# A 16-row copy of 1 KiB rows within SBUF, placed ahead of the alpha load on the ACT queue of a streaming add kernel

## Chip, cores and metric

The kernel runs on one core of a Trainium2 chip. The time is device microseconds of one execution; a kernel is quoted by the median of its runs. "Profile" and "trace" mean the record of one execution by the hardware profiler; its span is about 1.8 us shorter than the device time of the same execution. A run that is over 1.5% above the fastest run of the same kernel is marked "slow" and left out of the ratios.

Some words used below: SP, ACT, VectorE and PE are engines of the core. Transfers are issued on a queue, here that of SP or that of ACT; the core's 16 DMA engines carry out the transfers of both (the page gives both queues as shares of the same 16). A packet is one record of a DMA engine in the trace; here it is one row of a transfer, or a 4-byte completion, which reports that an engine's share of a transfer is done. A transfer lands when all its completions have arrived. A turn is the time from one packet of the ACT queue to the next on the same DMA engine. SBUF is the core's working memory, PSUM the memory that matmuls write to.

## The reference

```python
B, S, D = 512, 32, 640          # x, fx: bfloat16; alpha: one bfloat16 number
def reference(x, fx, alpha):
    return x + alpha * fx
```

Two inputs of 21 MB are read and one output of 21 MB is written. There is one multiply-add per element, so the kernel should run at the speed of its transfers.

## The kernel before

Each of the 128 partitions owns 81,920 elements. They are cut into five chunks of 16,384 elements, that is, rows of 32 KiB per partition and 4 MiB per transfer. All large loads and stores are issued on the SP queue. The one number alpha is loaded on the ACT queue, spread to 128 partitions by a one-column matmul and copied from PSUM to `a_f`, which every multiply-add needs.

```python
def alpha_to_lanes(nc, consts, psum, alpha, eng):
    a_1 = consts.tile([1, 1], alpha.dtype, name="a_1")
    eng.dma_start(out=a_1[:], in_=alpha[None, :])
    ones = consts.tile([1, P], alpha.dtype, name="ones")
    nc.vector.memset(ones[:], 1.0)
    a_ps = psum.tile([P, 1], F32, name="a_ps")
    nc.tensor.matmul(a_ps[:], ones[:], a_1[:], start=True, stop=True)
    a_f = consts.tile([P, 1], F32, name="a_f")
    nc.vector.tensor_copy(out=a_f[:], in_=a_ps[:])
    return a_f
# ... cut ...
    xs = ctx.enter_context(tc.tile_pool(name="xs", bufs=4))
    fs = ctx.enter_context(tc.tile_pool(name="fs", bufs=2))
    ctx.enter_context(tc.manual_schedule())
    a_f = alpha_to_lanes(nc, consts, psum, alpha, nc.scalar)
# ... cut: load_x, load_f, store issue on nc.sync; compute is x_t = f_t * a_f + x_t on VectorE ...
    load_x(0)
    load_f(0)
    load_x(1)
    load_f(1)
    load_x(2)
    compute(0)
    load_f(2)      # needs the buffer of f_t(0): waits for the end of compute(0)
    store(0)
    load_x(3)
    compute(1)
    load_f(3)
    store(1)
    load_x(4)      # needs the buffer of x_t(0): waits for store(0)
    compute(2)
    load_f(4)
    store(2)
    compute(3)
    store(3)
    compute(4, 2)  # in two halves
    store(4, 0, 2)
    store(4, 1, 2)
```

Of the kernel before, what the change touches and what calls it, by code (L numbers as in the profile page):

```python
# [1 line left out]

# [4 lines left out]

ACT = mybir.ActivationFunctionType
ALU = mybir.AluOpType
F32 = mybir.dt.float32  # L10
BF16 = mybir.dt.bfloat16

CHUNK = 16384


def alpha_to_lanes(nc, consts, psum, alpha, eng):

    P = nc.NUM_PARTITIONS
# [11 lines that stand above are left out]
@with_exitstack  # L30
def kernel(
    ctx: ExitStack,
    tc: tile.TileContext,
    x: bass.AP,
    fx: bass.AP,
    alpha: bass.AP,
    out: bass.AP,
):
    nc = tc.nc
    P = nc.NUM_PARTITIONS  # L40
    xv = x.flatten_outer_dims().rearrange("(p n) d -> p (n d)", p=P)
    fxv = fx.flatten_outer_dims().rearrange("(p n) d -> p (n d)", p=P)
    ov = out.flatten_outer_dims().rearrange("(p n) d -> p (n d)", p=P)
    F = xv.shape[1]
    K = F // CHUNK
    assert K * CHUNK == F and K == 5

    consts = ctx.enter_context(tc.tile_pool(name="consts", bufs=1))
    psum = ctx.enter_context(tc.tile_pool(name="psum", bufs=1, space=bass.MemoryType.PSUM))
    xs = ctx.enter_context(tc.tile_pool(name="xs", bufs=4))  # L50
    fs = ctx.enter_context(tc.tile_pool(name="fs", bufs=2))
    ctx.enter_context(tc.manual_schedule())

    a_f = alpha_to_lanes(nc, consts, psum, alpha, nc.scalar)
    xt, ft = {}, {}

    def load_x(k):
        xt[k] = xs.tile([P, CHUNK], x.dtype, tag="x", name="x_t")
        nc.sync.dma_start(out=xt[k][:], in_=xv[:, bass.ts(k, CHUNK)])  # L59

    def load_f(k):
        ft[k] = fs.tile([P, CHUNK], fx.dtype, tag="f", name="f_t")
        nc.sync.dma_start(out=ft[k][:], in_=fxv[:, bass.ts(k, CHUNK)])

    def compute(k, parts=1):
        n = CHUNK // parts
        for j in range(parts):
            s = bass.ts(j, n)
            nc.vector.scalar_tensor_tensor(  # L69
                out=xt[k][:, s],  # L70
                in0=ft[k][:, s],
                scalar=a_f[:],
                in1=xt[k][:, s],
                op0=ALU.mult,
                op1=ALU.add,
            )

    def store(k, j=0, parts=1):
        n = CHUNK // parts
        nc.sync.dma_start(  # L80
            out=ov[:, k * CHUNK + j * n : k * CHUNK + (j + 1) * n],
            in_=xt[k][:, bass.ts(j, n)],
# [8 lines that stand above are left out]
    load_f(2)  # L91
# [5 lines that stand above are left out]
    load_x(4)  # L97
# [5 lines that stand above are left out]
    compute(4, 2)  # L103
    store(4, 0, 2)
    store(4, 1, 2)


# [1 line left out]
_INS = ['x', 'fx', 'alpha']  # L109
_OUTS = [((512, 32, 640), 'bfloat16')]  # L110


# [23 lines left out]
```

## Time and profile before

| | before |
|---|---|
| time, median of the first 3 runs | 152.83 us (152.47 to 152.9) |
| span of the profiled run | 150.6 us |
| share of 16 DMA engines' span filled by the SP queue | 98.0% |
| bytes, mean rate | 62.92 MB, 418 GB/s |
| VectorE busy | 86.9 us, 58% |
| first multiply-add starts | 22.84 us |

These lines are from the page of the kernel before. The DMA row has one digit per fortieth of the span: the busy share of the 16 DMA engines in tenths. Below it are the counts of packets, and then the two queues, q1 (SP) and q10 (ACT).

```profile
DMA  6999999999999999799999999999999999999994
DMA packets 2306, 62.92 MB, mean 418 GB/s; under 512 B 258, under 2 KB 258, under 8 KB 258
q1 hardware_dynamic: 2304, 62.92, 98.0%
q10 hardware_dynamic: 2, 0.00, 0.0%
```

The reader sees a kernel bound by its DMA engines: they are full between the first and the last slice. The chain of waits of the same run (start, length, what) shows where that work is waited for.

```profile
1.16 21.55 DMA f_t<-in_fx_dram
22.84 17.30 DVE x_t L69
40.16 21.99 DMA f_t<-in_fx_dram
62.24 17.29 DVE x_t L69
79.55 41.16 DMA f_t<-in_fx_dram
120.91 8.75 DVE x_t L69
```

Three of the five loads of `f_t` carry the chain, the first, third and fifth; a multiply-add appears between them only where its end releases a buffer for a load (at 40.16 and 79.55). The load that begins at 40.16 is the third load of f, and it can only be issued when the first multiply-add has freed its buffer.

The timeline of the start (start, length, engine, line, operation, then in brackets the idle time before and what ended it) shows how alpha arrives.

```profile
0.73 0.38 SPq L59 DMA_DIRECT2D x_t<-in_x_dram  x1
0.73 0.49 ACTq L20 DMA_DIRECT2D a<-in_alpha_dram  x1
1.92 0.16 PE L24 MATMUL a_ps<-a,ones 1*128 1x1 bf16 x1 [1.92 <-DMA a<-in_alpha_dram]
2.11 0.16 DVE L26 COPY a_f<-a_ps 128x1 f32<-128x1 f32 x1 [1.13 <-PE a_ps L24]
22.84 17.28 DVE L69 SCALAR_TENSOR_TENSOR x_t<-f_t,a_f,x_t 128x16384 bf16<-128x16384 bf16 x1 [20.57 <-DMA f_t<-in_fx_dram]
```

Alpha's issue and the first load's issue begin together at 0.73. Alpha is on VectorE's side at 2.3 us, and VectorE then idles for 20.57 us until the first `f_t` lands.

### The profile page before, as it was taken

To read this page: it belongs to the slowest core of one execution; us is meant where nothing else is said; L and a number is where in the kernel's file an instruction comes from. 1 tells how busy PE (TensorE), PEld (TensorE's weight loads), DVE (VectorE), ACT (ScalarE), POOL (GpSimd) and SP (SyncE) were. 2 spreads that over 40 slices of the span, in tenths; PEclk is the share of its full clock that TensorE was granted. 3 is DMA by queue.
4 is the path that set the end of the run, shared out by engine and by line. 5 is a ranking of instruction groups with operands and counts; after the bars stand their busy time and mean duration, and the time that the engine had idled before them with its cause. 6 is when DMAs were issued, how large, how long until landed. Compare 5 with 4: busy or idle time off the path is not lost.

```text
span 150.6 us, 85 instructions
## 1 busy us (share of the span) xinstructions
PE 0.2 (0%) x1; PEld 0.1 (0%) x1; DVE 86.9 (58%) x8; POOL 0.2 (0%) x4
## 2 busy tenths in 40 slices
PE   0000000000000000000000000000000000000000
PEld 0000000000000000000000000000000000000000
DVE  0000009999679998499991006999900089997000
POOL 0000000000000000000000000000000000000000
DMA  6999999999999999799999999999999999999994
GB/s 200 444 453 435 418 418 418 418 444 453 444 453 435 418 418 418 339 444 470 418 418 418 418 418 435 435 435 453 426 435 444 418 418 435 435 435 405 426 444 205
DMA packets 2306, 62.92 MB, mean 418 GB/s; under 512 B 258, under 2 KB 258, under 8 KB 258
## 3 DMA queue, kind: packets, MB, share of 16 engines
q1 hardware_dynamic: 2304, 62.92, 98.0%
q10 hardware_dynamic: 2, 0.00, 0.0%
HBM read 41.94 MB, written 20.97 MB: 418 GB/s over the span
## 4 chain that ended last, share of the span: by engine, by line
DMA 56%; DVE 29%; DVEq 6%; issue 0%; SPq 0%
DMA f_t<-in_fx_dram 56%; DVE x_t L69 29%; DVEq L131 6%; SPq L59 0%; DVEq L69 0%
## 5 line engine op out<-in xcount | busy, mean ns | idle before, releaser
L69 DVE SCALAR_TENSOR_TENSOR x_t<-f_t,a_f,x_t 128x16384 bf16<-128x16384 bf16 (+1 forms) x6 | 86.6, 14439 | 49.5 <-DMA f_t<-in_fx_dram 49.5
L26 DVE COPY a_f<-a_ps 128x1 f32<-128x1 f32 x1 | 0.2, 159 | 1.1 <-PE a_ps L24 1.1
L22 DVE MEMSET ones<- 1x128 bf16 x1 | 0.2, 165 | 0.8 <-PEq L120 0.8
L24 PE MATMUL a_ps<-a,ones 1*128 1x1 bf16 x1 | 0.2, 159 | 1.9 <-DMA a<-in_alpha_dram 1.9
L120 POOL MEMSET const-bfloat16-1.0<- 128x1 bf16 x1 | 0.1, 102 | 0.0
L120 POOL MEMSET const-uint8-127<- 128x1 uint8 x1 | 0.1, 102 | 0.0
L24 PEld LDWEIGHTS <-ones 1*128 1x128 bf16 x1 | 0.1, 100 | 1.0 <-DVE ones L22 1.0
L120 POOL MEMSET const-float32-0.0<- 128x1 f32 x1 | 0.1, 99 | 0.2 <-issue 0.2
L120 POOL MEMSET const-float32-1.0<- 128x1 f32 x1 | 0.1, 99 | 0.0
## 6 DMA issues: line engine op xcount, KB each, us to landing
x_t<-in_x_dram SPq DMA_DIRECT2D x5, 4096.0 KB, 34.8
f_t<-in_fx_dram SPq DMA_DIRECT2D x5, 4096.0 KB, 32.1
out_dram<-x_t SPq DMA_DIRECT2D x4, 4096.0 KB, 36.5
out_dram<-x_t SPq DMA_DIRECT2D x2, 2048.0 KB, 15.2
a<-in_alpha_dram ACTq DMA_DIRECT2D x1, 0.0 KB
```

Source lines behind the costliest of these rows:

```text
L22: nc.vector.memset(ones[:], 1.0)
L24: nc.tensor.matmul(a_ps[:], ones[:], a_1[:], start=True, stop=True)
L26: nc.vector.tensor_copy(out=a_f[:], in_=a_ps[:])
L69: nc.vector.scalar_tensor_tensor(out=xt[k][:, s], in0=ft[k][:, s], scalar=a_f[:], in1=xt[k][:, s], op0=ALU.mult, op1=ALU.add,)
L120: nc = _bacc.Bacc("TRN2", target_bir_lowering=False, num_devices=1)
L131: with _tile.TileContext(nc) as tc:
```

## The change

A tile of 16 rows of 512 bfloat16 numbers is cleared and copied to another tile on the ACT queue, before alpha's load is issued there. Nothing reads the copy. It has the form of a warm-up of the queue; its effect on the result is none.

```diff
     ctx.enter_context(tc.manual_schedule())
 
+    w_a = consts.tile([16, 512], x.dtype, name="w_a")
+    nc.vector.memset(w_a[:], 0.0)
+    w_b = consts.tile([16, 512], x.dtype, name="w_b")
+    nc.scalar.dma_start(out=w_b[:], in_=w_a[:])
     a_f = alpha_to_lanes(nc, consts, psum, alpha, nc.scalar)
```

## The prediction

> **What bounds the kernel now.** The page gives a span of 150.6 us. In its forty slices the 16 DMA engines are in the top tenth nearly throughout, and the one big queue (q1) fills 98.0% of 16 engines' span: 62.92 MB at a mean of 418 GB/s. VectorE is busy 86.9 us (58%), nothing else matters. The chain of waits agrees: f_t loads 56%, then VectorE 29%; its last pieces are the landing of the fifth f_t at 120.72 us, two half multiply-adds (17.4 us), and the last store until 150.6. The DMA engines work through VectorE's part of the chain too (windows: share 1.01, 0.98, then 0.80 in the last 11 us, the drain).
>
> **What the change adds, removes, moves.** Nothing is removed; the order on SP, PE and POOL is the same, and on SP the same waits stand in front of the same transfers (DMA semaphores are handed out in rotation; none of the new waits can still be open at 40 us).
> - VectorE: a memset of 16 rows. That of `ones` took 0.165 us; estimate 0.2-0.3 us, while VectorE otherwise idles until 22.84.
> - ACT: its queue waits for that memset and issues the copy first. The alpha issue began at 0.73 us and took 0.49; I expect the copy's issue at about 1.1 and alpha's at 1.6.
> - Engines: 16 packets of 1 KiB, one per engine, and 16 completion packets. A 32 KiB packet takes 1.23 us in steady state; by bytes 1 KiB is 0.04 us, so my estimate is at most 0.1 us per engine, during start-up (windows: share 0.81 and 0.70 in the first 4 us).
> - Alpha lands later. Before, its matmul started at 1.92 us, 1.19 us after alpha's issue began. The Trainium skill (DMA: Bandwidth & Descriptors, "Queues, rings and completion order") says an engine goes round its queues packet by packet, so the ACT transfers pass between SP's packets instead of behind SP's whole queue. This trace doesn't show that yet: alpha's packets ran ahead of the first load. Estimate 2.8 us plus one to two 32 KiB packets: matmul at 3 to 6 us, a_f 0.2-0.4 us later.
>
> **How much is on the critical path.** The first multiply-add needs f_t(0), x_t(0) and a_f; f_t(0) releases it at 22.84, a_f is ready at 2.3. Alpha has about 20 us of slack and should lose 1 to 4. Only the DMA time counts: at most 0.1 us. SBUF addresses move by 2 KiB per partition, which should cost nothing.
>
> **Predicted time.** 152.9 us, range 152.2 to 153.7: before plus under 0.1 us, and the scatter of its runs (152.47 to 152.9). Faster by over 2%: 0.02. Within 2%: 0.95. Slower by over 2%: 0.03.
>
> **What would show each step.**
> - Page: DMA packets 2306 + 32 = 2338, q10 with 34; VectorE x9; q1 still about 98%.
> - Timeline: matmul at 3 to 6 us; first multiply-add still at about 22.9, released by f_t, not a_f.
> - Chain: same three members and shares; f_t(4) landing near 120.8.
> - Waits: SP's as before within a few tenths of us.
>
> **What would make it wrong.**
> - If alpha stood behind all loads already queued (five are issued in the first 3.2 us, about 50 us of traffic), the first multiply-add would be up to 25 us late; SP's waits on VectorE would grow and the engines run dry.
> - If a small packet put the engines out of step so that the rate changed for long: each 1% is 1.5 us.
> - If the copy's issue held up SP's first loads: 0.5 us at most.

## The result

The changed kernel takes 152.81 us (152.65 to 152.85, 4 runs), the kernel before 152.81 us (152.47 to 152.9, 4 runs). The ratio is 1.0002, with a 95% interval of 0.9985 to 1.0019. A ratio here is the mean time of one kernel's fast runs over that of the other's fast runs of the same rounds, so it is not quite the ratio of the quoted medians.

These lines of the changed kernel's page answer to those of before.

```profile
DMA  6999999999999999899999999999999999998993
DMA packets 2339, 62.93 MB, mean 417 GB/s; under 512 B 275, under 2 KB 291, under 8 KB 291
q1 hardware_dynamic: 2304, 62.92, 97.8%
q10 hardware_dynamic: 34, 0.02, 0.0%
```

The ACT queue has 34 packets instead of 2: 16 of 1 KiB, 16 completions, and alpha's two. (The thirty-third additional packet is an instruction fetch on another queue.) The SP queue is unchanged. The chain of waits has the same members at nearly the same times:

```profile
1.16 21.67 DMA f_t<-in_fx_dram
22.96 17.30 DVE x_t L74
40.28 22.04 DMA f_t<-in_fx_dram
62.41 17.30 DVE x_t L74
79.72 41.22 DMA f_t<-in_fx_dram
121.06 8.75 DVE x_t L74
```

The timeline of the start is where the change shows:

```profile
0.84 0.27 DVE L56 MEMSET w_a<- 16x256 uint32 x1 [0.84 <-PEq L125]
1.14 0.56 ACTq L58 DMA_DIRECT2D w_b<-w_a  x1
1.73 0.85 ACTq L20 DMA_DIRECT2D a<-in_alpha_dram  x1
10.37 0.16 PE L24 MATMUL a_ps<-a,ones 1*128 1x1 bf16 x1 [10.37 <-DMA a<-in_alpha_dram]
22.96 17.29 DVE L74 SCALAR_TENSOR_TENSOR x_t<-f_t,a_f,x_t 128x16384 bf16<-128x16384 bf16 x1 [12.24 <-DMA f_t<-in_fx_dram]
```

Alpha's matmul starts at 10.37 us instead of 1.92, which is 8.45 us later. The first multiply-add still starts on the landing of `f_t`, 0.12 us later than before. The idle time that VectorE spends just before it has only been split: 12.24 us there, and 9.31 us before the copy to `a_f`.

So the forecast of the time held, but one number in it did not: I had expected the matmul at 3 to 6 us. The experiments ask why alpha came so much later than I thought, how late it might have come without cost, and whether the copy itself costs anything. That the time was forecast rightly doesn't test the number for alpha: 12.24 us of VectorE's wait were left, so alpha could have come up to 12 us later still without delaying the first multiply-add.

### The profile page after: what moved, and what is told of

The parts are those of the page before. It is cut to its first block, busy times and chain, and to the rows that moved or that the text cites. A ratio compares the mean times of both kernels' runs of the same rounds, so it can differ in the third digit from the quotient of the medians.

```text
span 151.0 us, 87 instructions
## 1 busy us (share of the span) xinstructions
PE 0.2 (0%) x1; PEld 0.1 (0%) x1; DVE 87.1 (58%) x9; POOL 0.2 (0%) x4
## 3 DMA queue, kind: packets, MB, share of 16 engines
q1 hardware_dynamic: 2304, 62.92, 97.8%
## 4 chain that ended last, share of the span: by engine, by line
DMA 56%; DVE 29%; DVEq 6%; SPq 0%; issue 0%
DMA f_t<-in_fx_dram 56%; DVE x_t L74 29%; DVEq L136 6%; SPq L64 0%; DVEq L74 0%
## 5 line engine op out<-in xcount | busy, mean ns | idle before, releaser
L24 PE MATMUL a_ps<-a,ones 1*128 1x1 bf16 x1 | 0.2, 160 | 10.4 <-DMA a<-in_alpha_dram 10.4
```

## The experiments

Twelve experiments were run, all with correct results: ten variants, one of them on two chips, and the changed kernel once more. The kernel before was run beside them on the same chip, and each ratio is against those runs. Five of the twelve are a single run each; they serve for their traces, and their times are quoted only as a check.

### Why alpha is late

The trace records when each DMA packet moved its data. Taken from these records, the starts of the ACT queue's packets in us from the span's start (a range covers 16 engines):

```
                 copy data     copy completion  alpha data  alpha completion
before           -             -                1.58        1.59
change           5.91 - 6.62   7.16 - 7.87      8.62        9.84
late (no copy)   -             -                4.74        5.96
SP queue, both:  first 32 KiB packets from 1.74 on, the second ones from about 3.5 on;
                 median length of a 32 KiB packet 1.213
```

In the changed kernel alpha passes three further packets behind the first, and they stand about one large SP packet apart: 1.25, then about 1.2 to 1.3 (the records don't say which engine alpha's packet ran on), then 1.22 us. My estimate had counted one or two. The theory that follows from it: an engine gives each queue one packet in turn, a completion is a packet of its own, and on top of that the first ACT packet must wait for what SP has already handed to the engine. The rival is that the copy's own work or its mere presence delays alpha.

**Order swapped.** Alpha first, the copy behind it (this edit and the next two are shown against the changed kernel).

```diff
-    <the copy>
     a_f = alpha_to_lanes(nc, consts, psum, alpha, nc.scalar)
+    <the copy>
```

> The same copy, but behind alpha on the ACT queue instead of ahead of it. If alpha's lateness (matmul at 10.4 us after the change, 1.92 before) comes from its place in the queue and from arriving after the engines filled, the matmul is back at 1.9 to 2.1 us, and the copy itself still lands only at 6 to 9 us. If the copy's mere presence slows alpha, the matmul stays well over 3 us. Time the same as before within 0.5% in both.

```profile
1.95 0.16 PE L24 MATMUL a_ps<-a,ones 1*128 1x1 bf16 x1 [1.95 <-DMA a<-in_alpha_dram]
```

The matmul was at 1.95 us. The copy's data moved at 7.16 to 7.81 us and the copy landed at about 9.6 us, a little later than expected. The time was 152.99 us, one run, beside 153.35 for the kernel before. So the copy's presence doesn't delay alpha; being issued behind it does. The single time shows no loss.

**Alpha late, no copy.** Alpha's transfer waits for two memsets, so its issue begins at 1.16 us rather than 0.73.

```diff
-    nc.scalar.dma_start(out=w_b[:], in_=w_a[:])        # and w_b is gone
+    nc.vector.memset(a_1[:], 0.0)                      # in alpha_to_lanes, before the load
     eng.dma_start(out=a_1[:], in_=alpha[None, :])
```

> No copy at all; alpha's transfer only waits for two VectorE memsets, so it is issued at about 1.2 to 1.5 us instead of 0.73. Theory (a packet that comes after SP's first load was issued gets its first turn only after about four 32 KiB packets, and each further packet, the completion included, costs one more 32 KiB packet): alpha's data packet at about 6 us, its completion 1.2 us later, matmul at 7 to 8.5 us. Rival (the lateness is the copy's own cost, and alpha waits for the copy): matmul at 2.4 to 3 us. Time as before within 0.5%.

```profile
1.16 0.49 ACTq L21 DMA_DIRECT2D a<-in_alpha_dram  x1
6.33 0.16 PE L25 MATMUL a_ps<-a,ones 1*128 1x1 bf16 x1 [6.33 <-DMA a<-in_alpha_dram]
```

The matmul was at 6.33 us, between the two expectations but far from the rival's 3 us. An issue 0.43 us later costs alpha 4.4 us without any copy, because before the change alpha's packet left at 1.58 us, just ahead of the first SP packet at 1.74. So about half of the change's 8.45 us comes from losing that race, and about half from two more turns for the copy and an entry one turn later than here (why it was one turn later was not found). My theory had put alpha's data at 6 us and it came at 4.74: the wait for the first turn was over-sized by one packet. Time 152.43 us, one run.

**128 rows instead of 16.** The copy then has eight data packets of 1 KiB per engine.

```diff
-    w_a = consts.tile([16, 512], x.dtype, name="w_a")
+    w_a = consts.tile([128, 512], x.dtype, name="w_a")     # w_b0 likewise
```

> The copy with 128 rows of 1 KiB instead of 16, still ahead of alpha: 8 data packets per engine instead of 1. Theory (the engine takes one 1 KiB packet, then one 32 KiB packet, in turn): 7 more turns of 1.22 us, so the matmul at 18 to 20 us. Rival (an engine drains several small descriptors in one turn): matmul at 10.4 to 12 us. Time as before within 0.6% in both, as the first multiply-add starts at about 23 us.

```profile
17.58 0.16 PE L24 MATMUL a_ps<-a,ones 1*128 1x1 bf16 x1 [17.58 <-DMA a<-in_alpha_dram]
```

The matmul was at 17.58 us, a little under the theory's band and far from the rival's. The packet records say how the turns went: the first packets of the first five rows start at 5.91, 7.16, 8.41, 9.67 and 10.92 us, one turn of 1.25 us each. Between 12.2 and 13.0 us, on each engine, the sixth and the seventh follow each other within about 0.05 us. That is where the first load of x ends, so SP's packet between them is its own 4-byte completion: a turn is one packet, whatever its size. That short turn is 1.2 us less than a full one, which puts the matmul under my band. Time 153.31 us against 153.35, one run each.

**The first load in 8 KiB rows.** The changed kernel, with `load_x(0)` as four transfers.

```diff
-    load_x(0)
+    xt[0] = xs.tile([P, CHUNK], x.dtype, tag="x", name="x_t")
+    for q in range(4):
+        n = CHUNK // 4
+        nc.sync.dma_start(out=xt[0][:, bass.ts(q, n)], in_=xv[:, q * n : (q + 1) * n])
```

> The change as it is, but the first load of x in four transfers of 8 KiB rows instead of one of 32 KiB rows. Theory (each turn costs one SP packet of whatever size): a turn costs about 0.31 us instead of 1.22, so the matmul at 3.5 to 5.5 us. Rival (a fixed latency of an ACT transfer beside SP traffic): matmul still near 10 us. Time as before within 0.7%.

```profile
6.89 0.16 PE L24 MATMUL a_ps<-a,ones 1*128 1x1 bf16 x1 [6.89 <-DMA a<-in_alpha_dram]
```

The matmul was at 6.89 us, so neither expectation was met. The turns shrank as the theory says: from the copy's first data packet at 5.24 us to the last packet of alpha at 6.36 took 1.1 us, where the change took 3.9. But the first packet still had to wait until 5.24 us. The wait for the first turn is not a count of packets: about 10 SP packets per engine had started by then, instead of about 3. Time 152.69 us, one run.

**The first load in 2 KiB rows,** four such transfers and one of 24 KiB rows, to see what that first wait is.

```diff
-    load_x(0)
+    for lo, hi in ((0, 1024), (1024, 2048), (2048, 3072), (3072, 4096), (4096, CHUNK)):
+        nc.sync.dma_start(out=xt[0][:, lo:hi], in_=xv[:, lo:hi])
```

> The change, with the first load of x in four transfers of 2 KiB rows and one of 24 KiB rows, to see what sets how soon the first ACT packet gets a turn. With 32 KiB and with 8 KiB rows it was 4.8 and 4.1 us after the copy's issue, though engines had passed 3 packets in one case and about 10 in the other. Theory A (it waits for bytes that SP has already committed, about 64 to 96 KiB per engine; here only 16 KiB per transfer and engine): copy's packets at 2.5 to 4.0 us. Theory B (a fixed time of 3.6 to 4.8 us beside a busy queue): at 4.7 to 5.9 us. Time as before within 1% in both.

```profile
5.00 0.16 PE L24 MATMUL a_ps<-a,ones 1*128 1x1 bf16 x1 [5.00 <-DMA a<-in_alpha_dram]
```

The copy's data packets started at 3.32 to 3.9 us and the matmul at 5.00 us, as theory A has it. On the mean of the engines, SP had by then begun about 32 KiB, which is two of its small transfers. In the other runs it had begun 70 to 114 KiB where the ACT transfer was issued at about 1.15 us, 142 where it was issued at 2.60 (order swapped) and 166 where it was issued at 3.95 (the run with a hundred times the bytes, below). A fixed time is excluded by these traces. That an ACT transfer that arrives late waits for what SP has already committed fits them, but is not shown by itself. I did not find one number for how much that is; this part stays open. The kernel took 154.0 us in its one run, 1% more than the runs of before beside it (median 152.5), with its first `f_t` landing at 24.28 us. This was not repeated.

### How late alpha may come

**Alpha on the SP queue behind the second load of x,** with no copy:

```diff
-    a_f = alpha_to_lanes(nc, consts, psum, alpha, nc.scalar)
...
     load_x(1)
+    a_f = alpha_to_lanes(nc, consts, psum, alpha, nc.sync)
```

> The kernel before, with alpha's load moved from the ACT queue to the SP queue, behind the second load of x, to see how late alpha may come. It should land at about 32.5 us, so the first multiply-add starts at about 33 us instead of 22.9. Theory (what counts is whether the DMA engines still have work when the third load of f is issued; a first-in-first-out estimate from 9.83 us per 4 MiB load and 17.29 us per multiply-add gives room until an alpha at 33 us): time as before, 152.8, at most +0.6 us. Rival (the room is the 20.5 us that VectorE waits for f_t, as my prediction had it): 10 us later, about 163 us.

```profile
32.47 17.29 DVE L68 SCALAR_TENSOR_TENSOR x_t<-f_t,a_f,x_t 128x16384 bf16<-128x16384 bf16 x1
```

The first multiply-add started at 32.47 us. Two of the five runs were slow (156.19 and 156.41); the three fast ones were 153.84, 155.61 and 156.08 us, against 152.89 (152.62 to 154.21) for the kernel before. The ratio of the fast runs is 1.0196 (1.0136 to 1.0255), at the limit of 2% and so unclear. The rival's +10 us is excluded. The theory's "at most +0.6" is wrong too. Because of the scatter it was run again on another chip:

> The kernel with alpha behind the second load of x on the SP queue again, on another chip perhaps, since its times scattered (153.8 to 156.4) where others agree within 1 us. If it lies on the edge at which the engines just run dry before the third load of f, +1 to +3.5 us and again a wide scatter; if that scatter was the chip's, it settles near +1 us (its profile then: third f_t landing 1.2 us later). The rival of my prediction, +10 us, is already excluded.

Again the times scattered: 153.23, 153.94 and 154.53 us, and a slow run of 155.77, against 152.50 (152.25 to 152.91); ratio of the fast runs 1.0086 (1.0039 to 1.0133). In both profiles the third `f_t` lands about a microsecond later than before (63.3 and 63.1 us, before 62.1). The engines hardly stop, but the load comes so late that its packets begin on engines with nothing else queued: in the first of the two runs it was issued at 49.78 us, and its first packets, from 50.76 us on, took 1.5 to 1.9 us, where the median is 1.213. This is about the edge. The fast runs of the two series cover 2.2 and 1.3 us; the kernel before covered 1.6 and 0.7 beside them, and 2.1 on a third chip. In each series the profiled run was the fastest one, so the traces don't show where the others lost their time; this stays open.

**Alpha behind the second load of f,** ten microseconds later:

```diff
     load_f(1)
+    a_f = alpha_to_lanes(nc, consts, psum, alpha, nc.sync)
```

> The same with alpha behind the second load of f: it should land at about 42.3 us, the first multiply-add at about 43. Theory: beyond 33 us the time follows alpha one for one, so +9 to +11 us, about 163 us, with the DMA engines idle for about 10 us before the third load of f. Rival (room is 20.5 us): +20 us, about 173.

The time was 163.8 us (163.51 to 164.38), ratio 1.0706 (1.0653 to 1.0759), slower. The start of the first multiply-add in the timeline, the issue of the third load of f, and the DMA row of the page:

```profile
42.25 17.29 DVE L68 SCALAR_TENSOR_TENSOR x_t<-f_t,a_f,x_t 128x16384 bf16<-128x16384 bf16 x1
59.56 0.33 SPq L62 DMA_DIRECT2D f_t<-in_fx_dram  x1
```
```profile
DMA  7999899999994028989999999999999999999994
```

The hole in slices 13 to 16 is the loss. The table of stretches (length, the busy time of the engines, the granted clock, the DMA share, GB/s) gives its size:

```profile
40.00:51.00 11.00, 0.16 (x1) 0.00 (x0) 8.91 (x2) 0.00 (x0) 1.00 0.98 423
51.00:60.00 9.00, 0.00 (x0) 0.00 (x0) 9.00 (x2) 0.00 (x0) 1.00 0.00 0
60.00:74.00 14.00, 0.00 (x0) 0.00 (x0) 14.00 (x1) 0.00 (x0) 1.00 1.00 374
```

From 51 to 60 us not a byte moved while VectorE worked on the first chunk, because `load_f(2)` was waiting for that chunk's buffer. The multiply-add was 19.4 us late (42.25 against 22.84), and the kernel lost 0.0706 of about 153 us, or 10.8. So 8.6 us of the delay was free. In the kernel before, the same load had its buffer 19.4 us earlier:

```profile
40.16 0.33 SPq L63 DMA_DIRECT2D f_t<-in_fx_dram  x1
```

**The change grown threefold and eightfold in rows:** three copies of 128 rows ahead of alpha.

```diff
-    w_a = consts.tile([16, 512], x.dtype, name="w_a")
+    w_a = consts.tile([128, 512], x.dtype, name="w_a")
     nc.vector.memset(w_a[:], 0.0)
-    w_b = ...; nc.scalar.dma_start(out=w_b[:], in_=w_a[:])
+    w_b0, w_b1, w_b2 = ...; the same copy into each of the three
```

> The change grown: three copies of 128 rows of 1 KiB ahead of alpha, 0.4 MB in all. By bytes they are about 1 us of the engines. Theory of turns: 24 data and 3 completion packets per engine, then alpha's two, 28 further turns of 1.22 us after about 6 us: matmul at 39 to 42 us, first multiply-add at about 41, and by the estimate of first-in-first-out that is 7 to 9 us more than before, 160 to 162 us. Rival (only bytes count): about 153.9 us. If small packets are drained several per turn: matmul under 16 us and time about 153.9.

```profile
38.03 0.16 PE L24 MATMUL a_ps<-a,ones 1*128 1x1 bf16 x1 [38.03 <-DMA a<-in_alpha_dram]
38.42 17.29 DVE L78 SCALAR_TENSOR_TENSOR x_t<-f_t,a_f,x_t 128x16384 bf16<-128x16384 bf16 x1
```
```profile
DMA  7999999999999089989999999999999999999993
```

The time was 160.25 us (159.34 to 160.8), ratio 1.0463 (1.0403 to 1.0523), slower. The matmul came about a microsecond before the band, for the short turns seen above. The first multiply-add was 15.6 us late and the kernel lost 0.0463 of about 153 us, or 7.1; again 8.5 us of the delay was free. Two ways of making alpha late, through two queues, give the same room. The copies' own engine time is not to be taken off first: it only moves the start of the hole, from 51.3 to 52.6 us (last packet before it). SP's third load of x was issued late here (13.38 us, before 2.71), after a wait of 10.6 us for the first load of x; SP had other loads queued, and the engines stayed full. Copies of 0.4 MB, worth about 1 us of the engines by their bytes, cost seven times that, and they cost it through alpha: the same hole stands in the DMA row.

**Two copies of 128 rows,** which make alpha later than the first `f_t` but not late enough to starve the engines.

> Two copies of 128 rows of 1 KiB ahead of alpha, so that alpha is later than the f_t(0) that used to release the first multiply-add, but well before the DMA engines run dry. From the run with three copies, whose second one was complete at 25.5 us: matmul at 27.5 to 28.5, first multiply-add at about 28, 5 us later than in the kernel before, and now released by a_f. Theory (room up to 30 to 33 us): time as before plus the copies' own engine time of under 1 us, ratio 1.000 to 1.008. Rival (VectorE's wait for f_t(0) is all the room): +5 us, ratio 1.03.

```profile
27.77 0.16 PE L24 MATMUL a_ps<-a,ones 1*128 1x1 bf16 x1 [27.77 <-DMA a<-in_alpha_dram]
28.17 17.29 DVE L76 SCALAR_TENSOR_TENSOR x_t<-f_t,a_f,x_t 128x16384 bf16<-128x16384 bf16 x1
```

The time was 153.2 us (152.99 to 153.74) against 152.5, ratio 1.0035 (1.0005 to 1.0066): 0.5 us, for a multiply-add that is 5.3 us late and was released by alpha, not by `f_t`. The copies' 0.26 MB would take 0.6 us at 418 GB/s, so the delay itself cost nothing that these runs can show.

### What the copy's own traffic costs

**A hundred times the bytes, after alpha.** Two copies of 128 rows of 6 KiB, 1.57 MB in all, behind alpha on the ACT queue.

```diff
     a_f = alpha_to_lanes(nc, consts, psum, alpha, nc.scalar)
+    w_a = consts.tile([P, 3072], x.dtype, name="w_a")
+    nc.vector.memset(w_a[:], 0.0)
+    w_b = consts.tile([P, 3072], x.dtype, name="w_b")
+    for h in range(2):
+        nc.scalar.dma_start(out=w_b[:], in_=w_a[:])
```

> Alpha first, then two copies of 128 rows of 6 KiB within SBUF on the ACT queue, 1.57 MB in all, so that alpha is not late and only the copies' DMA time counts. Theory (the engines are the bound, so their time is added in full): 1.57 MB at the 418 GB/s of the loads is 3.8 us, so +3.2 to +4.6 us, 156 to 157.5 us. By the same rate the change's own 16 KiB is 0.04 us, too small to see. Rival (copies within SBUF overlap with the loads, or fall into gaps): under +1 us.

```profile
q10 hardware_dynamic: 290, 1.57, 2.4%
```

The time was 156.13 us (155.95 to 156.32) against 152.89, ratio 1.0200 (1.0153 to 1.0247), about 3.1 us. The interval is clear of 1 but not of 2%, so the verdict is "unclear". The point is just under the theory's band and well over the rival's. The copies' packets took 2.4% of the engines' span, 3.8 us per engine by the packet records. So most of the engines' time is added, and the interval (2.3 to 3.8 us) reaches up to all of it. The change's own copy took 0.055 us per engine by its packet records (46 ns of data and 9 ns of completion), far under what a comparison of runs resolves.

**The changed kernel in five rounds:**

> The changed kernel again, in five rounds, for a narrower interval. Theory: at most 0.1 us (0.07%) of engine time is added, so the ratio is between 0.999 and 1.002; the matmul again at 9.5 to 11 us. A ratio over 1.003 or under 0.997 would say that something else moves.

The times were 153.03 us (152.69 to 153.59) against 153.16 (152.52 to 154.62), ratio 0.9981 (0.9942 to 1.0021). The point lies just outside what I had expected, but this chip scattered more and the interval is wider than in the first comparison; it contains 1. The matmul was at 10.29 us. The first result, 1.0002, stays the sharper one.

## Why the prediction was right, and where it was not

- **The bound.** Right. The DMA engines are full before and after (98.0% and 97.8%), and the run with 1.57 MB of additional traffic shows that most of the added engine time is paid: 3.1 us of 3.8.
- **The time.** Right: 152.81 us measured, 152.9 predicted. The only addition to the critical resource, under 0.1 us by my estimate, is 0.055 us per engine by the packet records. No comparison of runs here could resolve it, so "costs nothing" means "nothing seen within 0.2%".
- **Packets and instructions.** Right: 34 packets on the ACT queue, one memset of 0.27 us more, issues of the copy and of alpha at 1.14 and 1.73 us.
- **The last `f_t`.** Right: it landed at 120.94 us, predicted near 120.8.
- **When alpha lands.** Wrong in size: "2.8 us plus one to two 32 KiB packets: matmul at 3 to 6 us", and it was at 10.37. The mechanism was right, and the term of the sum that failed is the number of packets waited for. The Trainium skill (DMA: Bandwidth & Descriptors, "Queues, rings and completion order") says that an engine goes round its queues at packet granularity, and these traces agree, with turns of 1.25 us. What I left out is that the copy's data, the copy's completion, alpha's data and alpha's completion each take a turn of their own, which makes three turns after the first, 3.9 us here. I also left out how long the first of them waits before its first turn: it moved 4.8 us after its issue, where alpha alone, ahead of SP's first packet, had needed 0.85. What sets this wait stays open; with less committed by SP it was shorter (2.2 us behind 2 KiB rows).
- **The slack.** Sufficient but mis-stated: "about 20 us of slack" was the wait of VectorE. From the two losses I estimate room until the first multiply-add starts at about 31 us (22.84 plus 8.5); the runs at 28.17 us (no loss seen) and 32.47 us (a small one) agree. So alpha's matmul could have started at about 31 and not only at 22. What must not run dry is the DMA engines. In the kernel before, `load_f(2)` is issued at 40.16 us while the last of the loads issued ahead of it lands at 51.9. A first-in-first-out estimate had put the edge at 33 us; the edge worked out from the runs is earlier by about 2 us. That is about the time in which a load that finds the engines empty gets under way: with alpha behind the second load of f, it was issued at 59.56 us, its first packets began at 60.5 to 61.0, and they took 1.5 to 2.2 us instead of 1.213.
- **The ways to be wrong.** The first one I named, engines running dry behind a late alpha, is real. It needed an alpha about 20 us later than the change makes it. The other two did not occur: the mean rate was 417 GB/s (before 418), and SP's first five loads were issued at the same times within 0.02 us.

Neither the change nor any variant is faster than the kernel before beyond what the runs resolve, and no run pointed to a version that would be. The one thing to keep from the original is its order: alpha issued at once.

## What to carry to other kernels

A small transfer on a second queue beside large packets pays in turns, not in bytes: count its data packets per engine and its completion, add those of everything ahead of it on its queue, multiply by the time of one packet of the busy queue, and add the wait before the first turn, 3.6 to 4.8 us behind 32 KiB rows here (the packet that ends this wait is not counted again). Issue the number that everything needs before the bulk loads fill the engines, and put nothing ahead of it that isn't needed. Then judge its lateness by when the bound resource runs dry, not by how long its consumer happens to idle: here 5 us of delay after the consumer's idle time was free and 19 us cost 11.

## What the Trainium skill lacked or had wrong

- DMA: Bandwidth & Descriptors, "Queues, rings and completion order", gives a turn as a whole packet, typically of about 9 to 17 descriptors. On these two queues a turn was one row: a single 1 KiB row against a single 32 KiB row. Of the seven steps between eight rows, six were about 1.25 us, and one, behind a 4-byte completion of the SP queue, about 0.05.
- The same page doesn't say what a transfer on a second queue waits for before its first turn. It was 0.85 us from issue to data ahead of SP's first packet, 3.6 to 4.8 us behind 32 KiB rows, 4.1 us behind 8 KiB rows, and 2.2 us behind 2 KiB rows.
- The same page, "Issuing engines are not separate DMA queues", says that issuing on several engines only saves the sequencer's issue time. For a small transfer it saves far more: alpha on the ACT queue, even behind the copy, reached its matmul at 10.4 us, and on the SP queue behind three and four loads at 32.1 and 41.9 us.
